# A planner that is told how long DMA transposes take, and loads of a pipeline's start held back and cast on the way in: a two-layer attention and feed-forward kernel

## Chip, cores, metric

One core of one Trainium2 chip. The metric is the device time of one execution in microseconds (us). Each kernel was run several times, and every kernel that is compared ran on the same chip in turns with the kernel before. All runs used here are of the normal ("fast") state. A ratio is the mean time of one kernel's fast runs over the mean of the other's of the same rounds, with a 95% interval, so it is not quite the ratio of the medians quoted beside it. The rounds ran on different chips, so kernels of different rounds are compared by their ratios to before.

## The reference

Two identical layers on x of 1 x 2048 x 576 (bfloat16), cut to what matters:

```
x = x + attention(layernorm(x))     # 32 heads of 18, causal, window of 256 keys
x = x + feed_forward(layernorm(x))  # 576 -> 4608, gelu, 4608 -> 576, biases b1, b2
# and both once more with the same weights
```

## The kernel before

The tokens go through in chunks of 512 (four tiles of 128 rows); two layers of four chunks make eight, k = 0 to 7. For a chunk there are these pieces, and the kernel interleaves the pieces of neighbouring chunks so that TensorE always has something to do:

- `qkv(k)`: projections of the normalised and transposed chunk (`xnTa`), 24 groups of 5 matmuls; results are cast by VectorE (DVE) and transposed by DMA into `qT`, `kT`;
- `E(k)`: attention in eight groups of four heads, in two halves (k,0) and (k,1): scores on TensorE, exp on ScalarE (ACT), causal and window masks on GpSimd (POOL, `affine_select`), values matmul on TensorE, normalisation on DVE into `attq`;
- `tail(k)`: `attq` is transposed by DMA into `attT`, the output projection is added to the residual `x_res`, and the result is normalised and transposed (`xnTm`);
- `G(k,h)` and `mm2(k,h)`, h = 0, 1: the two halves of the feed-forward, first matmul with GELU on ACT, second matmul added to `x_res`.

Almost no engine order is written by hand (only ACT's work, and scores and first feed-forward matmuls among each other, keep the order in which the program states them). Every instruction is a task with a believed duration (`cost`), a believed extra time until its result is there (`lat`) and a priority. A list scheduler in the host program takes, again and again, the task that could start first by these beliefs, and of equals the one with the lower priority number. The order that comes of it is fixed in the program; semaphores keep it correct. So a wrong belief never gives a wrong result: it puts an instruction too early in the queue of its engine, which then stands and waits with work behind it that was ready.

```python
            free[t.eng] = st + t.cost
            t.end = st + t.cost + t.lat
    ...
        # every DMA transpose, in ln_norm_T, qkv and tail:
        add("sp", lambda e: e.dma_start_transpose(...), ..., dma="t", ring=8, cost=1.3, lat=1.4, prio=...)
    ...
    # the start: x, q/k/v weights, x again, wo, all at once
    x_load(0, n0, [], 4.0, -10)               # plain loads into x_in, a view of hT
    for n, w in enumerate("qkv"):
        dma("act", wqkv[...], ..., lat=7.0 + 3 * n, prio=-10, fifo="act")
    for a in range(n0, NT, 4):
        x_load(a, min(4, NT - a), ["wkA"], 4.0 + (a - n0) * 0.75, -10)
    dma("act", wo_sb[...], ..., lat=14.0, ...)
    ...
    for t in range(NT):                       # residual in float32, cast by POOL
        add("pool", lambda e, t=t: e.tensor_copy(x_res[:, t, :], x_in[:, t, :]), ...)
    for i in range(n0):
        qkv(0, i, -5)
    for t in range(n0, NT):                   # statistics of all later tiles
        ln_stats(t, -1, x_in, f"xin{t}")
    ln1(1, -0.9)
    ...
    for _ in range(NB1):                      # feed-forward weights, as soon as q of chunk 0 is there
        w1_load(0, [f"q{n0 - 1}"])
    w2_load(0, 0, [f"q{n0 - 1}"])
    ...
    # in tail(k), after the normalisation of a tile:
            add("pool", lambda e, t=t: e.tensor_tensor(x_res[:, t, :], x_res[:, t, :], b2bc[:, :], ALU.add),
                reads=["b2"], writes=X(t), cost=1.4, prio=prio + 0.9)
```

The softmax here doesn't subtract the row's maximum and nothing guards it: scores larger than these inputs give would overflow.

## Time and profile before

| | before |
|---|---|
| median of 3 runs | 1006.06 us (1005.98 to 1006.28) |
| TensorE busy (profiled run) | 927.4 of 1007.7 us |
| TensorE waits for `attT` | 16.8 us in 9 pieces |
| first matmul | 15.01 us |

How to read it: PE is TensorE's matmuls, PEld its weight loads; a busy share near 1 means that only idle time, and time in which TensorE runs at a lower clock, can be won. The page's first lines, and the row of its 40-slice table that gives the granted clock in tenths (each slice is 25 us):

```profile
span 1007.7 us, 22352 instructions
PE 927.4 (92%) x9312; PEld 584.9 (58%) x9312; DVE 311.9 (31%) x771; ACT 586.2 (58%) x705; POOL 378.4 (38%) x519
...
PE   3596799899999999899998999999999999999998
...
PEclk9786799999999999999998999999999999999999
```

The first five slices belong to the ramp, the start of the run until its stages repeat: PE shows 3, 5, 9, 6 and 7 there, at a lower clock. From the sixth slice on PE shows 8 or 9 in every slice.

The view of waits, for PE alone (what ended each idle piece; us in total, times, longest):

```profile
engine line waited for: us in total, times, longest us
PE ps L519 <- DMA xnTa<-xn: 25.3, 4, 15.0
PE ps L519 <- DMA attT<-attq: 16.8, 9, 3.6
PE ps L589 <- ACT pT L598: 12.2, 22, 1.3
```

L519 is a matmul of `qkv` or of the output projection; the tile name tells which. The 25.3 us for `xnTa` lie in the ramp (15.0 of them before the first matmul); the waits for `attT` are nine pieces in eight chunks, spread over the run after 133 us. The timeline of PE in one of the repeating stages shows what such a wait does (start, length, what, and in brackets the idle time before it):

```profile
773.24 0.29 PE L525 MATMUL ps<-wqkv,xnTa 128*128 128x288 bf16 x1
...
773.85 0.29 PE L525 MATMUL ps<-wqkv,xnTa 128*128 128x288 bf16 x1
776.18 0.67 PE L519 MATMUL ps<-wo_sb,attT 128*128 128x288 bf16 x4 [2.04 <-DMA attT<-attq]
...
777.63 0.45 PE L525 MATMUL ps<-wo_sb,attT 128*128 128x288 bf16 x1
```

TensorE stands for 2.04 us until the first `attT` transpose lands, then runs the first tile. SP's queue in the same trace has the four `attT` transposes issued from 771.64 us. The last matmul of `qkv` ended at 774.14 us (773.85 + 0.29), 2.5 us after the issue; the data came 4.5 us after it. The planner believed 1.3 + 1.4 = 2.7 us (`cost` and `lat`).

### The profile page before, as it was taken

The numbers are of one execution on the slowest core, as the hardware profiler recorded it, in microseconds if no ns is written. First come the engines' busy times: TensorE is split into PE (matmuls) and PEld (weight loads), VectorE is DVE, ScalarE is ACT, GpSimd is POOL, SyncE is SP. The second block draws the span as 40 slices with busy tenths as digits, with TensorE's granted clock in tenths as the row PEclk, the third lists the DMA queues.
The fourth block names the chain that finished last, engine by engine and source line by source line (L and its number), as shares of the span: only waits on it lengthen the run. The fifth ranks groups of instructions, "written<-read, shape, count | busy, mean of one in ns | idle before, by whom it ended". The sixth has DMA issues, their size and how long they took to land.

```text
span 1007.7 us, 22352 instructions
## 1 busy us (share of the span) xinstructions
PE 927.4 (92%) x9312; PEld 584.9 (58%) x9312; DVE 311.9 (31%) x771; ACT 586.2 (58%) x705; POOL 378.4 (38%) x519
## 2 busy tenths in 40 slices
PE   3596799899999999899998999999999999999998
PEld 2363556556565656656575565755566565656556
DVE  4742611342136211534036130361114410132001
ACT  0356568577753777447761687627774377852531
POOL 8445724354333434425153161533333342541000
PEclk9786799999999999999998999999999999999999
DMA  9925220974268251881628633484517725074540
GB/s 252 273 45 89 54 72 25 199 187 131 72 150 164 75 163 39 180 184 41 183 70 170 148 108 94 120 177 103 166 48 170 143 66 183 25 194 122 184 129 25
DMA packets 226757, 126.60 MB, mean 126 GB/s; under 512 B 141792, under 2 KB 226528, under 8 KB 226656
## 3 DMA queue, kind: packets, MB, share of 16 engines
q1 hardware_dynamic: 219456, 122.20, 49.0%
q10 hardware_dynamic: 2432, 2.65, 0.9%
q0 software_dynamic: 4768, 0.31, 0.8%
q8 instruction: 74, 1.21, 0.5%
q14 instruction: 27, 0.22, 0.1%
HBM read 90.10 MB, written 2.36 MB: 92 GB/s over the span
## 4 chain that ended last, share of the span: by engine, by line
PE 68%; DMA 4%; DVE 3%; ACT 3%; issue 1%; POOL 1%; SPq 0%; DVEq 0%
PE ps L737 26%; PE ps L712 24%; PE ps L519 6%; PE ps L636 6%; PE ps L589 4%; DMA attT<-attq 3%; ACT pT L598 2%; PE ps L525 1%; DVE x_res L670 1%; DMA xnTm<-xn 1%; POOL rstd L460 1%; DVE xn L470 1%; ACT hT L716 1%; DVE st_all L447 0%; ACT L753 0%
## 5 line engine op out<-in xcount | busy, mean ns | idle before, releaser
L619 POOL TENSOR_SCALAR_AFFINE_SELECT pT<-pT 128x512 bf16<-128x512 bf16 (+1 forms) x368 | 278.1, 778 | 409.6 <-ACT pT L598 385.3
L598 ACT ACTIVATE pT<-ps 128x1024 bf16<-128x1024 f32 (+2 forms) x384 | 347.2, 971 | 133.6 <-PE ps L589 132.2
L716 ACT ACTIVATE hT<-ps,b1col 128x512 bf16<-128x512 f32 x288 | 196.6, 687 | 262.6 <-PE ps L712 262.4
L737 PE MATMUL ps<-w_sb,hT 128*128 128x288 bf16 x2304 | 314.2, 286 | 6.7 <-DVE x_res L670 5.6
L712 PE MATMUL ps<-xnTm,w_sb 128*128 128x512 bf16 x1440 | 320.1, 379 | 0.1
L737 PEld LDWEIGHTS ps<-w_sb,hT 128*128 128x128 bf16 x2304 | 210.3, 97 | 80.7 <-issue 20.5
L712 PEld LDWEIGHTS ps<-xnTm,w_sb 128*128 128x128 bf16 x1440 | 139.6, 98 | 158.6 <-issue 0.2
L670 DVE TENSOR_TENSOR x_res<-ps,x_res 128x288 f32<-128x288 f32 x160 | 71.0, 450 | 399.9 <-PE ps L737 362.4
L519 PE MATMUL ps<-wqkv,xnTa 128*128 128x288 bf16 x768 | 127.7, 297 | 29.7 <-DMA xnTa<-xn 25.3
L636 PEld LDWEIGHTS ps<-vA,pT 128*128 128x128 bf16 x2880 | 94.4, 96 | 29.1 <-issue 11.2
L519 PEld LDWEIGHTS ps<-wqkv,xnTa 128*128 128x128 bf16 x768 | 73.1, 101 | 58.5 <-issue 18.8
L636 PE MATMUL ps<-vA,pT 128*128 128x20 bf16 x2880 | 100.5, 172 | 5.3 <-POOL pT L619 3.8
L589 PE MATMUL ps<-qT,kT 32*128 32x384 bf16 (+2 forms) x1408 | 76.5, 285 | 18.7 <-ACT pT L598 12.2
L555 DVE CAST qn<-ps 128x288 bf16<-128x288 f32 x128 | 57.0, 452 | 55.2 <-PE ps L525 50.0
L519 PE MATMUL ps<-wo_sb,attT 128*128 128x288 bf16 x256 | 45.9, 313 | 16.8 <-DMA attT<-attq 16.8
L525 PE MATMUL ps<-wqkv,xnTa 128*128 128x288 bf16 x192 | 56.8, 296 | 0.0
L589 PEld LDWEIGHTS ps<-qT,kT 32*128 32x128 bf16 x1408 | 22.6, 93 | 53.9 <-issue 30.0
L694 POOL TENSOR_TENSOR x_res<-x_res,b2bc 128x576 f32<-128x576 f32 x32 | 45.0, 1409 | 15.1 <-DVE xn L470 13.9
L673 DVE TENSOR_TENSOR xn<-ps,x_res 128x288 bf16<-128x288 f32 x32 | 14.6, 457 | 114.7 <-PE ps L737 114.7
L470 DVE TENSOR_SCALAR xn<-x_res,mv_all,rstd 128x576 bf16<-128x576 f32 x60 | 43.1, 723 | 22.1 <-POOL rstd L460 10.4
L458 POOL TENSOR_SCALAR vtmp<-mv_all 128x1 f32<-128x1 f32 (+1 forms) x43 | 8.6, 200 | 103.6 <-DVE mv_all L449 101.2
L519 PEld LDWEIGHTS ps<-wo_sb,attT 128*128 128x128 bf16 x256 | 26.2, 106 | 30.7 <-DMA attT<-attq 20.6
(29 smaller groups left out, 281.5 us busy)
## 6 DMA issues: line engine op xcount, KB each, us to landing
w_sb<-in_B_w_dram SPq DMA_DIRECT2D x144, 288.0 KB, 5.2
w_sb<-in_B_w_dram SPq DMA_DIRECT2D x72, 512.0 KB, 4.2
w_sb<-in_B_w_dram SPq DMA_DIRECT2D x72, 64.0 KB, 3.9
hT<-in_A_x_dram SPq DMA_DIRECT2D x4, 576.0 KB, 6.3
out_dram<-xn SPq DMA_DIRECT2D x16, 144.0 KB, 1.8
wqkv<-in_A_wqkv_dram ACTq DMA_DIRECT2D x3, 576.0 KB, 7.4
wo_sb<-in_A_wo_dram ACTq DMA_DIRECT2D x1, 576.0 KB, 9.6
xnTa<-xn SPq DMA_TRANSPOSE x32, 3.9
```

Source lines behind the costliest of these rows:

```text
L470: add("dve", lambda e: e.tensor_scalar(xn[:, sl, 0:D], s[:, t, :], mv_all[:, t, 0:1], rstd[:, t:t + 1], op0=ALU.subtract, op1=ALU.mult), r ...
L519: ins = e.matmul(bank(bs[o])[:, 0:n], lhs(o, c, full), rhs(o, c, full), start=(c == 0), stop=False)
L525: ins = e.matmul(bank(bs[o])[:, 0:n], lhs(o, 4, full), rhs(o, 4, full), start=False, stop=True)
L555: add("dve", lambda e, o=o, b=bs[o], qv=qv: e.tensor_copy(qv[:, o * 16:(o + 1) * 16, 0:DH], bank(b)[:, 0:HB].rearrange("p (h d) -> p h d", ...
L589: ins = e.matmul(two(bs[j // 2])[:, j % 2, col:col + nq * 128], kT[32 * j:32 * j + 32, g, (T0 + so) % KS, :], qT[32 * j:32 * j + 32, g, qo ...
L598: add("act", lambda e, h2=h2: e.activation(pT[:, sl, 2 * h2:2 * h2 + 2, lo:hi], two(bs[h2])[:, :, lo:hi], ACT.Exp, scale=SCALE), reads=[bs ...
L619: add("pool", lambda e, ap=ap, pat=pat, sgn=sgn, kind=kind: e.affine_select(ap, ap, pattern=pat, compare_op=(ALU.is_ge if kind == "d" else ...
L636: ins = e.matmul(bank(B_O)[:, o:o + VW], pT[:, sl, j, col + qi * 128:col + (qi + 1) * 128], vA[:, (T0 + so) % VS, 4 * g + j, :], start=(fi ...
L670: add("dve", lambda e: e.tensor_tensor(x_res[:, t, sl], bank(b)[:, 0:HB], x_res[:, t, sl], ALU.add), reads=[b], writes=[f"x{t}h{hh}"], cos ...
L712: ins = e.matmul(bank(bk)[:, 0:n], w1_sb[:, sl, col:col + 128], xnTm[:, k % 2, c, 0:n], start=(c == 0), stop=(c == KD - 1))
L716: add("act", lambda e, f=f, fl=fl, bk=bk: e.activation(hT[:, fl, 0:n], bank(bk)[:, 0:n], ACT.Gelu_apprx_tanh, bias=b1col[:, f:f + 1]), rea ...
L737: ins = e.matmul(bank(b)[:, 0:HB], hT[:, fl, i * 128:(i + 1) * 128], w2_sb[:, fl, hh * HB:(hh + 1) * HB], start=(fl == 0), stop=(fl == NFH ...
```

## The change

Its intent: give the planner a truer picture of DMA, and clear the start of the kernel of transfers that nobody needs yet. The core of the diff:

```diff
+            if t.dma is not None:                       # one DMA queue in the plan
+                dma_free = max(dma_free, st + t.cost) + t.move
+                t.lat = max(t.lat, dma_free + 1.3 - st - t.cost)
             t.end = st + t.cost + t.lat
...
     def dma(q, out_, in_, ...):
-        add(q, ..., **kw)                               # latencies given by hand
+        add(q, ..., lat=1.3, move=n / 270e3, **kw)      # n: bytes written
...
-            ... dma="t", ring=8, cost=1.3, lat=1.4, ...             # xn, q, k transposes
+            ... dma="t", ring=8, cost=1.3, lat=2.5, move=0.6, ...
-            reads=rd + ["aqd"], ... lat=1.4, prio=prio - 0.1)       # attT transposes
+            reads=rd + ["aqd"], ... lat=4.0, move=0.6, prio=prio - 0.1)
...
+    def x_load(a, cnt, reads, prio):                    # bf16 -> float32 on the way, issued by POOL
+        dma("pool", x_res[:, a:a + cnt, :], x_dram[...], reads=reads, ..., cls="xr", ...)
-    (x of all chunks, wo, q/k/v weights at once; POOL casts; statistics of all tiles in one block)
+    w_load(0); w_load(1)
+    x_load(chunk 1, [f"xa{n0 - 1}"])   # after chunk 0's last transpose
+    w_load(2, ["xa0"])                 # v weights after its first
+    x_load(chunk 0, [f"k{n0 - 1}"])
+    stats0(1)                          # statistics chunk by chunk
+    # in E(0): wo after group 0, x of chunk 2 after group 1, w1 blocks after groups 3, 5, 7
+    # in G(0,0): w2 pair by pair behind the GELUs, x of chunk 3 after the seventh GELU
-            ... x_res + b2 on POOL: prio=prio + 0.9
+            ... prio=prio + 3
-        memset of qn: all columns
+        memset of qn: only the padding columns
```

More of the change, by code (lines that the diff above doesn't have):

```diff
@@ L158 @@
 class Task:
-    __slots__ = ("idx", "eng", "fn", "reads", "writes", "cost", "lat", "prio", "dma", "ring", "handles", "alloc",
+    __slots__ = ("idx", "eng", "fn", "reads", "writes", "cost", "lat", "prio", "dma", "ring", "handles", "alloc", "move",
                  "npred", "succ", "ready", "end", "plain")
@@ L194, in __init__, with add @@
         self.fifo_last = {}
-    def add(self, eng, fn, reads=(), writes=(), dma=None, ring=4, cost=0.1, lat=0.1, prio=0.0, alloc=(), fifo=None, plain=False, after=()):
+    def add(self, eng, fn, reads=(), writes=(), dma=None, ring=4, cost=0.1, lat=0.1, prio=0.0, alloc=(), fifo=None, plain=False, after=(), move=0.0):
         t = Task(idx=len(self.tasks), eng=eng, fn=fn, reads=tuple(reads), writes=tuple(writes), cost=cost, lat=lat, prio=prio,
                  dma=dma, ring=ring, alloc=tuple(alloc), handles=tuple({r for r in tuple(reads) + tuple(writes) if isinstance(r, Bank)}),
-                 plain=plain)
+                 plain=plain, move=move)
         pred = set()
@@ L260, in schedule @@
         order = []
+        dma_free = 0.0
         n = len(self.tasks)
@@ L398, in dma @@
     def dma(q, out_, in_, reads=(), writes=(), cls="w", ring=8, **kw):
-        add(q, lambda e: e.dma_start(out_, in_), reads=reads, writes=writes, dma=cls, ring=ring, **kw)
-    def x_load(a, n, reads, lat, prio):
-        dma("sp", x_in[:, a:a + n, :], x_dram[a * P:(a + n) * P, :].rearrange("(t p) d -> p t d", p=P), reads=reads,
-            writes=[f"xin{t}" for t in range(a, a + n)], cls="x", ring=4, cost=0.6, lat=lat, prio=prio)
+        n = 2 if cls != "xr" else 4
+        for s in out_.shape:
+            n *= s
@@ L405, in build_kernel @@
+        add(q, lambda e: e.dma_start(out_, in_), reads=reads, writes=writes, dma=cls, ring=ring, lat=1.3, move=n / 270e3, **kw)
     n0 = CH[0][2]
-    x_load(0, n0, [], 4.0, -10)
-    for n, w in enumerate("qkv"):
-        dma("act", wqkv[:, 0:4, n * D:(n + 1) * D], A_wqkv[0:512, n * D:(n + 1) * D].rearrange("(c p) d -> p c d", p=P),
-            writes=[f"w{w}A"], lat=7.0 + 3 * n, prio=-10, fifo="act")
-        dma("act", wqkv[0:64, 4, n * D:(n + 1) * D], A_wqkv[512:576, n * D:(n + 1) * D], writes=[f"w{w}B"], lat=7.0 + 3 * n, prio=-10,
-            fifo="act")
-        if PAIR:
-            dma("act", wqkv[64:128, 4, n * D:(n + 1) * D], A_wqkv[512:576, n * D:(n + 1) * D], writes=[f"w{w}C"], lat=7.0 + 3 * n,
-                prio=-10, fifo="act")
@@ L415, in build_kernel @@
-    for a in range(n0, NT, 4):
-        x_load(a, min(4, NT - a), ["wkA"], 4.0 + (a - n0) * 0.75, -10)
-    dma("act", wo_sb[:, 0:4, :], A_wo[0:512, :].rearrange("(c p) d -> p c d", p=P), writes=["woA"], lat=14.0, prio=-10, fifo="act")
-    dma("act", wo_sb[0:64, 4, :], A_wo[512:576, :], writes=["woB"], lat=14.0, prio=-10, fifo="act")
-    if PAIR:
-        dma("act", wo_sb[64:128, 4, :], A_wo[512:576, :], writes=["woC"], lat=14.0, prio=-10, fifo="act")
+    dma("sp", x_in[:, 0:n0, :], x_dram[0:n0 * P, :].rearrange("(t p) d -> p t d", p=P), writes=[f"xin{t}" for t in range(n0)], cls="x",
+        ring=4, cost=0.6, prio=-10)
@@ new lines, in w_load @@
+    def w_load(n, reads=()):
+        w = "qkv"[n]
+        dma("act", wqkv[:, 0:4, n * D:(n + 1) * D], A_wqkv[0:512, n * D:(n + 1) * D].rearrange("(c p) d -> p c d", p=P), reads=reads,
+            writes=[f"w{w}A"], cost=0.6, prio=-10, fifo="act")
+        dma("act", wqkv[0:64, 4, n * D:(n + 1) * D], A_wqkv[512:576, n * D:(n + 1) * D], reads=reads, writes=[f"w{w}B"], cost=0.6, prio=-10,
+            fifo="act")
+    def x_load(a, cnt, reads, prio):
+        dma("pool", x_res[:, a:a + cnt, :], x_dram[a * P:(a + cnt) * P, :].rearrange("(t p) d -> p t d", p=P), reads=reads,
+            writes=[r for t in range(a, a + cnt) for r in X(t)], cls="xr", ring=8, cost=1.2, prio=prio)
@@ L422, in build_kernel @@
+    w_load(0)
+    w_load(1)
     add("pool", lambda e: e.memset(nhalf[:, :], -0.5), writes=["nhalf"], cost=0.1, prio=-10)
@@ L426, in build_kernel @@
     for i in range(NQN):
-        add("pool", lambda e, i=i: e.memset(qn[:, i, :], 0.0), writes=[f"qn{i}h{h}" for h in range(2)], cost=1.0, prio=-9)
+        add("pool", lambda e, i=i: e.memset(qn[:, i, :].rearrange("p (h e) -> p h e", e=32)[:, :, DH:32], 0.0),
+            writes=[f"qn{i}h{h}" for h in range(2)], cost=0.5, prio=-9)
     if not PAIR:
@@ L433, in build_kernel @@
     dma("pool", b2bc[:, :], bass.AP(tensor=B_b2.tensor, offset=B_b2.offset, ap=[[0, P], [1, D]]), writes=["b2"], cls="b", ring=2,
-        cost=1.0, lat=4.0, prio=-7)
+        cost=1.0, prio=-7)
     def load_b1(e):
@@ L479, in ln_norm_T @@
         add("sp", lambda e: e.dma_start_transpose(dst[:, :, i * 128:(i + 1) * 128], xn[:, sl, :]),
-            reads=rd, writes=[f"{dname}{i}"], dma="t", ring=8, cost=1.3, lat=1.4, prio=prio)
+            reads=rd, writes=[f"{dname}{i}"], dma="t", ring=8, cost=1.3, lat=2.5, move=0.6, prio=prio)
     w1n = [0]
@@ L493, in w1_load @@
         dma("sp", w1_sb[:, sl, 0:2048].rearrange("p (c f) -> p c f", c=4), B_w1[0:512, cols].rearrange("(c p) f -> p c f", p=P),
-            reads=reads, writes=[f"w1a{sl}"], cls="w1", cost=0.5, lat=4.0, prio=prio)
+            reads=reads, writes=[f"w1a{sl}"], cls="w1", cost=0.5, prio=prio)
         if PAIR:
@@ L498, in w1_load, with w2_load @@
                 dma("sp", w1_sb[64 * b:64 * b + 64, sl, 2048:2304].rearrange("p (a f) -> p a f", a=2), src[:, b],
-                    writes=[f"w1b{sl}_{b}"], cls="w1", cost=0.5, lat=4.0, prio=prio)
+                    writes=[f"w1b{sl}_{b}"], cls="w1", cost=0.5, prio=prio)
         else:
-            dma("sp", w1_sb[0:64, sl, 2048:2560], B_w1[512:576, cols], reads=["w1Z"], writes=[f"w1b{sl}_0"], cls="w1", cost=0.5, lat=4.0,
+            dma("sp", w1_sb[0:64, sl, 2048:2560], B_w1[512:576, cols], reads=["w1Z"], writes=[f"w1b{sl}_0"], cls="w1", cost=0.5,
                 prio=prio)
-    def w2_load(hf, prio, reads=()):
+    def w2_load(hf, prio, gate=False):
         for pr in range(NFH // 2):
@@ L507, in w2_load @@
             dma("sp", w2_sb[:, 2 * pr:2 * pr + 2, :], B_w2[f0 * P:(f0 + 2) * P, :].rearrange("(w p) d -> p w d", p=P),
-                reads=reads, writes=[f"w2s{pr}"], cls="w2", ring=9, cost=0.6, lat=4.0, prio=prio)
+                reads=[f"h{2 * pr}"] if gate else [], writes=[f"w2s{pr}"], cls="w2", ring=9, cost=0.6, prio=prio)
     def two_out(lhs, rhs, n, reads, prio, after=()):
@@ L562, in qkv @@
                 add("sp", lambda e, dst=dst, sl=sl: e.dma_start_transpose(dst, qn[:, sl, :]),
-                    reads=[f"qn{sl}h0", f"qn{sl}h1"], writes=[dn], dma="t", ring=8, cost=1.3, lat=1.4, prio=prio)
+                    reads=[f"qn{sl}h0", f"qn{sl}h1"], writes=[dn], dma="t", ring=8, cost=1.3, lat=2.5, move=0.6, prio=prio)
     def units_of(k):
@@ L683, in tail @@
             add("sp", lambda e, i=i: e.dma_start_transpose(attT[:, :, i * 128:(i + 1) * 128], attq[:, i, :]),
-                reads=rd + ["aqd"], writes=[f"aT{i}"], dma="t", ring=8, cost=1.3, lat=1.4, prio=prio - 0.1)
+                reads=rd + ["aqd"], writes=[f"aT{i}"], dma="t", ring=8, cost=1.3, lat=4.0, move=0.6, prio=prio - 0.1)
         for i in range(nt):
@@ L694, in tail @@
             add("pool", lambda e, t=t: e.tensor_tensor(x_res[:, t, :], x_res[:, t, :], b2bc[:, :], ALU.add),
-                reads=["b2"], writes=X(t), cost=1.4, prio=prio + 0.9)
+                reads=["b2"], writes=X(t), cost=1.4, prio=prio + 3)
     def G_part(k, hf, prio):
@@ L743, in mm2 @@
             if fin:
-                dma("sp", out_dram[t * P:(t + 1) * P, :], xn[:, osl, 0:D], reads=[f"xn{osl}", f"xd{osl}"], cls="o", ring=4, cost=0.5, lat=2.0,
+                dma("sp", out_dram[t * P:(t + 1) * P, :], xn[:, osl, 0:D], reads=[f"xn{osl}", f"xd{osl}"], cls="o", ring=4, cost=0.5,
                     prio=prio)
@@ L769, in build_kernel, with stats0, wo_load @@
         ln_norm_T(i, i, xnTa, "xa", -6, x_in, f"xin{i}")
-    for t in range(NT):
-        add("pool", lambda e, t=t: e.tensor_copy(x_res[:, t, :], x_in[:, t, :]), reads=[f"xin{t}"], writes=X(t), cost=0.7,
-            prio=-2 if t >= n0 else -4)
+    x_load(CH[1][1], CH[1][2], [f"xa{n0 - 1}"], -6)
+    w_load(2, ["xa0"])
     for i in range(n0):
         qkv(0, i, -5)
-    for t in range(n0, NT):
-        ln_stats(t, -1, x_in, f"xin{t}")
+    x_load(0, n0, [f"k{n0 - 1}"], -4)
+    def stats0(k):
+        l, t0, nt = CH[k]
+        for t in range(t0, t0 + nt):
+            ln_stats(t, 4 * k - 5)
+    stats0(1)
     ln1(1, -0.9)
-    add("pool", lambda e: e.memset(fence[:, :], 0.0), reads=[f"xin{t}" for t in range(NT)], writes=[f"h{f}" for f in range(NFH)],
+    add("pool", lambda e: e.memset(fence[:, :], 0.0), reads=[f"xin{t}" for t in range(n0)], writes=[f"h{f}" for f in range(NFH)],
         cost=0.1, prio=-4)
-    for _ in range(NB1):
-        w1_load(0, [f"q{n0 - 1}"])
-    w2_load(0, 0, [f"q{n0 - 1}"])
+    def wo_load():
+        dma("act", wo_sb[:, 0:4, :], A_wo[0:512, :].rearrange("(c p) d -> p c d", p=P), reads=["aq0"], writes=["woA"], cost=0.6, fifo="act")
+        dma("act", wo_sb[0:64, 4, :], A_wo[512:576, :], reads=["aq0"], writes=["woB"], cost=0.6, fifo="act")
+    later = [k for k in range(2, NK) if CH[k][0] == 0]
     for k in range(NK + 1):
@@ L790, in build_kernel @@
             E(k, range(0, 4), b - 0.5)
+            if k == 0:
+                wo_load()
+                kk = later[0]
+                x_load(CH[kk][1], CH[kk][2], ["aq1"], 0)
+                stats0(kk)
+                w1_load(-1, ["aq3"])
         if k >= 2:
@@ L795, in build_kernel @@
             G_part(k - 1, 0, b + 1)
+        if k == 1:
+            w2_load(0, 1, True)
+            for n, kk in enumerate(later[1:]):
+                x_load(CH[kk][1], CH[kk][2], [f"h{6 + 6 * n}"], b + 2)
+                stats0(kk)
         if not last:
             E(k, range(4, 8), b + 1.5)
+            if k == 0:
+                w1_load(-1, ["aq5"])
+                w1_load(-1, ["aq7"])
         if k >= 1:
@@ L805, in build_kernel @@
             tail(k, b + 1.9)
+            if k == 0:
+                w1_load(-1, ["xm0_0"])
         if k >= 1:
```

## The prediction

> **What bounds it now.** TensorE: the page has PE busy 927 of 1007.7 us. A new order can win only the 80 us of idle and the time at a low clock. Idle by stretches (busy time per window): first matmul at 15.0 us; 1.9 to 34.0; 13.4 to 53.8 at clock 0.56; 9.4 to 94.2 at 0.80; 6.7 to 133.4 (the first feed-forward matmul) at 0.78; 34 after. The ramp thus holds 46 us of idle and some 15 us (estimate from busy time and clock) lost to slow matmuls (0.44 us against 0.29 for a 128x288). The Trainium skill ("TensorE: Matmul & The Clock Gate", Part 1) says the clock halves after an idle window of about 3.4 us; the trace agrees: 0.50 after the 7.8 us wait at 44 us.
>
> **Where the ramp loses.** (a) The first matmul waits for a transpose issued at 9.6 us, with v weights, wo and more x tiles in flight; PE waits again (1.8 us) at 22. (b) VectorE does all 12 later tiles' statistics in one block (30 to 41 us), so chunk 1's transposes are issued at 44.6, behind thirteen w1/w2 loads (35.5 to 44.5 us, 350 to 390 GB/s): the 7.8 us wait. "DMA: Bandwidth & Descriptors" (Queues, rings and completion order) says each SDMA engine consumes an issuer's ring in order; the late transposes agree. (c) E(0), chunk 0's attention, has 35.8 us of exp on ScalarE but takes 60. (d) From 103 to 116 us four x_res+b2 adds (1.4 us each) on POOL stand between the mask selects.
>
> **What the change does.** v weights wait for the first transpose, wo for the first attention group; w1 goes block by block during E(0), w2 pair by pair during the first feed-forward. Later x chunks come by casting DMAs on POOL's queue: 16 casts of 0.62 us go (10 us, off the path), about 1 us of descriptor work per load (estimate from b2's 0.8 us) comes, written bytes double. Statistics go chunk by chunk; b2 adds move behind the masks. The planner believes longer transposes (2.5, 4.0 us; trace: 2.6 to 3.9) and a DMA queue, so it should fill the wait before the output projection.
>
> **Sum (estimates).** First matmul at 11.5, no second wait: -4. The 7.8 us wait and its cold matmuls: -9. Tighter E(0), warmer clock, freer masks: -9. First feed-forward matmul at 111 instead of 133. Afterwards the waits for attT (16.8 us in nine pieces) and their neighbours halve: -7. Against it: nine w2 loads (2.6 MB), four w1 blocks (2.4 MB) and an x chunk in the first feed-forward's 18 us, near 390 GB/s: +3; planner accidents +2. Total -24.
>
> **Prediction: 982 us, 8 in 10 between 964 and 998.** Faster by over 2% (under 985.9): 0.60; within 2%: 0.37; slower: 0.03.
>
> **What would show it.** The 15.0 and 7.8 us waits for xnTa become about 11 and under 2; idle before the first feed-forward matmul falls from 46 to about 28 us, and the clock of slices 2 to 5 rises. Waits for attT after the ramp fall below 9 us. PE busy falls to about 915. POOL's cast group disappears. DMA share nears 1 in the first feed-forward.
>
> **What would make it wrong.** SP issues in order: a held-back load released later than planned blocks transposes behind it. Slow casting DMAs (before has none) would delay chunk 1. Exp (36+23 us for E(0) and half of E(1)) may bound the ramp and keep the clock low. Work moved out of the ramp may only return later. If the steady order does not improve: about 990.

## The result

| | before | after |
|---|---|---|
| median | 1006.02 us (4 runs) | 990.62 us (989.61 to 993.21, 4 runs) |
| ratio | | 0.9855 (0.9832 to 0.9879) |
| TensorE busy | 927.4 us | 919.6 us |
| first matmul | 15.01 us | 14.47 us |
| TensorE waits for `attT` | 16.8 us | 4.3 us |

The changed kernel ran once more in a later round: 990.75 us, ratio 0.984 (0.9817 to 0.9863). It is 15.4 us faster by the first medians, inside the predicted range. It is not faster by over 2%, to which the prediction had given 0.60; "within 2%" had 0.37.

The profile after, the same lines (the line numbers have moved: L523 was L519, L593 was L589):

```profile
span 991.5 us, 22315 instructions
PE 919.6 (93%) x9263; PEld 583.4 (59%) x9312; DVE 317.2 (32%) x771; ACT 585.8 (59%) x705; POOL 369.4 (37%) x507
...
PE   4676699999999999999999999999999999999998
...
PEclk9795799999999999999999999999999999999999
```

The view of waits of after, PE alone (columns as before):

```profile
PE ps L593 <- ACT pT L602: 18.3, 28, 1.4
PE ps L523 <- DMA xnTa<-xn: 14.7, 2, 14.5
PE ps L640 <- POOL pT L623: 7.6, 6, 3.0
PE ps L640 <- DVE attq L655: 4.5, 1, 4.5
PE ps L523 <- DMA attT<-attq: 4.3, 4, 1.7
```

The waits for `attT` are nearly gone. In the ramp only the wait before the first matmul is left of those for `xnTa`, but waits for exp, masks and `attq` have come in their place, and the clock digits of the first slices are no better. In the stage shown above the projection now comes later in TensorE's order, behind more `qkv` groups, and nothing waits:

```profile
764.90 0.29 PE L529 MATMUL ps<-wqkv,xnTa 128*128 128x288 bf16 x1
765.26 0.66 PE L523 MATMUL ps<-wo_sb,attT 128*128 128x288 bf16 x4
765.76 0.29 PE L529 MATMUL ps<-wo_sb,attT 128*128 128x288 bf16 x1
```

SP issued the first of these transposes at 760.87 us in this trace, 4.4 us ahead of the projection's first matmul.

**Where the 16 us came from.** Two traces can only be compared between points at which the same work has been done. The obvious mark, the start of the first feed-forward (133.36 us before, 124.93 after), is not such a point: before, 100 of chunk 2's 120 `qkv` matmuls had been done by the first GELU, after, only 50; at 0.12 us each (0.65 us for four and 0.29 for the fifth, which overlap to 0.61 a group) the missing 50 are 6 us of work. At the first matmul of `mm2(0,1)` the counts of matmuls of all kinds agree again, in these two traces and in those of all experiments (but for the matmuls that e10 adds). The ramp is counted up to this mark from here on. It started at 213.18 us before and at 209.45 after. So the ramp gave 3.7 us, and the repeating stages the other 12.5 of the 16.2 us between these two profiled runs. The windows between such marks, before and after (length, busy time with counts for PE, PEld, DVE, ACT, POOL, then clock, DMA share, GB/s):

```profile
core 0: us, PE busy (x) PEld busy (x) DVE busy (x) ACT busy (x) POOL busy (x), PEclk, DMA share, GB/s
15.01:34.39 19.38, 17.48 (x124) 12.54 (x124) 13.45 (x36) 0.00 (x0) 9.21 (x17) 1.00 1.47 206
34.39:94.83 60.44, 37.61 (x540) 23.73 (x540) 25.24 (x70) 35.82 (x48) 32.17 (x46) 0.71 0.56 132
94.83:153.61 58.78, 52.11 (x519) 30.79 (x519) 23.93 (x56) 36.07 (x43) 27.91 (x36) 0.86 0.30 70
153.61:213.18 59.57, 55.00 (x590) 34.34 (x583) 19.57 (x47) 37.92 (x45) 27.16 (x36) 1.00 0.66 146
213.18:1007.70 794.52, 765.16 (x7555) 483.43 (x7548) 222.40 (x545) 475.12 (x570) 268.98 (x360) 0.99 0.48 123
```

The same windows of after:

```profile
14.47:32.07 17.60, 17.55 (x124) 12.75 (x124) 10.61 (x25) 0.00 (x0) 0.82 (x1) 1.00 1.11 204
32.07:88.26 56.19, 37.94 (x540) 24.19 (x540) 25.83 (x69) 35.61 (x49) 32.75 (x46) 0.72 0.62 132
88.26:145.36 57.10, 45.66 (x465) 25.51 (x468) 25.24 (x58) 35.91 (x43) 28.83 (x37) 0.80 0.59 142
145.36:209.45 64.09, 60.60 (x639) 39.58 (x633) 24.95 (x59) 37.85 (x45) 28.53 (x38) 1.00 0.67 145
209.45:991.50 782.05, 757.86 (x7511) 481.31 (x7548) 223.44 (x544) 475.13 (x570) 269.02 (x360) 1.00 0.50 126
```

The marks are: first matmul; first exp; first exp of chunk 1; first `mm2(0,0)` matmul; first `mm2(0,1)` matmul; end. The third window is 1.7 us shorter with 50 fewer `qkv` matmuls in it (the table shows 54 fewer records, as some are missing), and its idle time went up from 6.7 to 11.4 us; the fourth is 4.5 us longer because the 50 matmuls came back there. The last window is 12.5 us shorter. (49 of the 9,312 matmul records are missing from this trace of after, so its split into busy and idle is not exact; the lengths are. The second trace of the same kernel, after_again, is complete and shows 11.2 us of idle time in the third window.)

How far can one profile be trusted? The profiled run of after was the slowest of its four, that of after_again the fastest of its four. They differ by 0.8 us at `mm2(0,1)` and by 2.7 us from there to the end, and the waits for `attT` are 4.3 us in one and 0.6 in the other. Differences of that size between single profiles show nothing.

### The profile page after: what moved, and what is told of

It reads as the page before. It is cut to its first block, busy times and chain, and to the rows that moved or that the text cites. A ratio compares the mean times of both kernels' runs of the same rounds, so it can differ in the third digit from the quotient of the medians.

```text
span 991.5 us, 22315 instructions
## 1 busy us (share of the span) xinstructions
PE 919.6 (93%) x9263; PEld 583.4 (59%) x9312; DVE 317.2 (32%) x771; ACT 585.8 (59%) x705; POOL 369.4 (37%) x507
## 4 chain that ended last, share of the span: by engine, by line
PE 80%; DMA 5%; DVE 4%; ACT 4%; issue 3%; POOL 3%; SPq 1%; DVEq 0%; POOLq 0%
PE ps L741 28%; PE ps L716 27%; PE ps L523 10%; PE ps L640 7%; PE ps L593 6%; ACT pT L602 3%; DMA attT<-attq 2%; PE ps L529 2%; DVE x_res L674 1%; DVE st_all L451 1%; POOL rstd L464 1%; POOL pT L623 1%; DMA xnTa<-xn 1%; DMA x_res<-in_A_x_dram 1%; ACT hT L720 1%
## 5 line engine op out<-in xcount | busy, mean ns | idle before, releaser
L716 PE MATMUL ps<-xnTm,w_sb 128*128 128x512 bf16 x1391 | 312.6, 379 | 3.2 <-ACT pT L602 0.6
L523 PE MATMUL ps<-wqkv,xnTa 128*128 128x288 bf16 x768 | 127.1, 296 | 18.7 <-DMA xnTa<-xn 14.7
L640 PEld LDWEIGHTS ps<-vA,pT 128*128 128x128 bf16 x2880 | 94.6, 97 | 38.1 <-issue 15.5
L523 PEld LDWEIGHTS ps<-wqkv,xnTa 128*128 128x128 bf16 x768 | 73.7, 101 | 44.8 <-issue 15.0
L593 PE MATMUL ps<-qT,kT 32*128 32x384 bf16 (+2 forms) x1408 | 77.6, 289 | 23.6 <-ACT pT L602 18.3
L593 PEld LDWEIGHTS ps<-qT,kT 32*128 32x128 bf16 x1408 | 22.7, 93 | 60.5 <-issue 28.8
L474 DVE TENSOR_SCALAR xn<-x_res,mv_all,rstd 128x576 bf16<-128x576 f32 x60 | 46.8, 796 | 26.2 <-POOL rstd L464 13.8
L451 DVE BATCH_NORM_STATS2 st_all<-x_res 128x6 f32<-128x288 f32 x120 | 50.7, 445 | 13.7 <-DMA x_res<-in_A_x_dram 12.4
L698 POOL TENSOR_TENSOR x_res<-x_res,b2bc 128x576 f32<-128x576 f32 x32 | 45.3, 1416 | 13.9 <-DVE xn L474 12.5
L650 DVE RECIPROCAL rinv<-ps 128x16 f32<-128x16 f32 x64 | 16.4, 257 | 95.6 <-PE ps L640 95.5
```

Source lines behind the costliest of these rows:

```text
L451: add("dve", lambda e, i=i, s=s: e.bn_stats(st_all[:, t, i, :], s[:, t, i * HB:(i + 1) * HB]), reads=res, writes=[f"st{t}_{i}"], cost=0.43 ...
L523: ins = e.matmul(bank(bs[o])[:, 0:n], lhs(o, c, full), rhs(o, c, full), start=(c == 0), stop=False)
L593: ins = e.matmul(two(bs[j // 2])[:, j % 2, col:col + nq * 128], kT[32 * j:32 * j + 32, g, (T0 + so) % KS, :], qT[32 * j:32 * j + 32, g, qo ...
L640: ins = e.matmul(bank(B_O)[:, o:o + VW], pT[:, sl, j, col + qi * 128:col + (qi + 1) * 128], vA[:, (T0 + so) % VS, 4 * g + j, :], start=(fi ...
L716: ins = e.matmul(bank(bk)[:, 0:n], w1_sb[:, sl, col:col + 128], xnTm[:, k % 2, c, 0:n], start=(c == 0), stop=(c == KD - 1))
```

## The experiments

Three questions were left: which part of the change gave the gain of the repeating stages; why the ramp, of which 22 us were expected (at the first feed-forward matmul), gave 3.7; and whether the parts that did not pay can be made to. The marks of all kernels (us in the profiled run; start of the first matmul, of the first exp, of chunk 1's first exp, and of `mm2(0,1)`, and the time from there to the end):

| kernel | first matmul | first exp | E(1) starts | mm2(0,1) | rest | `attT` waits | ratio to before |
|---|---|---|---|---|---|---|---|
| before | 15.0 | 34.4 | 94.8 | 213.2 | 794.5 | 16.8 | 1 |
| after | 14.5 | 32.1 | 88.3 | 209.4 | 782.0 | 4.3 | 0.9855 |
| after again | 14.4 | 32.3 | 87.6 | 208.6 | 779.3 | 0.6 | 0.984 |
| e1 planner alone | 21.5 | 38.1 | 89.2 | 207.2 | 780.3 | 3.0 | 0.9817 |
| e2 loads alone | 14.4 | 37.7 | 90.5 | 212.5 | 796.9 | 17.0 | 1.001 |
| e3 three latencies alone | 15.2 | 36.1 | 92.4 | 211.4 | 779.1 | 1.1 | 0.9843 |
| e5 `attT` latency alone | 14.8 | 34.1 | 95.4 | 213.3 | 780.5 | 1.9 | 0.9881 |
| e6 the two others alone | 15.0 | 34.2 | 93.0 | 211.3 | 791.0 | 16.0 | 0.9986 |
| e4 after, chunk 1 free | 14.4 | 32.8 | 83.3 | 204.6 | 780.2 | 1.9 | 0.9806 |
| e7 e4, b2 adds late | 14.5 | 32.6 | 83.9 | 207.1 | 775.5 | 2.2 | 0.9766 |
| e8 e7, b1 load late | 16.8 | 33.7 | 83.6 | 206.0 | 774.9 | 2.2 | 0.9745 |
| e9 e1, b2 adds late | 21.8 | 38.9 | 89.9 | 210.6 | 775.0 | 3.4 | 0.9787 |

All ran in five rounds, and all but one gave the correct result (the one is said).

### e1_planner: the planner's part on the old loads

```diff
 (kernel before)
+            if t.dma is not None:
+                dma_free = max(dma_free, st + t.cost) + t.move
+                t.lat = max(t.lat, dma_free + 1.3 - st - t.cost)
+        kw["lat"] = 1.3            # in dma(), with move = bytes / 270e3
-  lat=1.4                          # the transposes
+  lat=2.5, move=0.6  (attT: lat=4.0, move=0.6)
```

> The kernel before with the planner's part alone: the DMA queue in the plan, bytes as time, transposes believed to take 2.5, 2.5 and 4.0 us; loads, casts and gates as before. Theory P (the change gains in the repeating stages, because matmuls are put before the output projection): 12 us of the 15.5 come from the planner, so about 994 us, and the waits for attT after the ramp fall from 16.8 us to under 6; the start of chunk 1's second feed-forward half (mm2 (0,1), 213.2 us in before) moves by under 4 us. Rival L (the gain comes from the staged loads of the ramp): under 4 us faster, 1002 us or more.

Measured: 989.59 us against 1007.56, ratio 0.9817 (0.9792 to 0.9842), waits for `attT` 3.0 us. The planner's part alone gives the whole gain; its interval overlaps that of the full change. Theory L falls. Theory P holds for the repeating stages (780.3 us against 794.5), but its bound on the ramp does not: the planner alone moved `mm2(0,1)` by 6.0 us, not under 4. It did so although its first matmul came at 21.5 us, 6.5 us later than before. So a later first matmul need not make the kernel later, although an earlier one was one of the terms of the prediction. (The order differs from before in other places too, so this does not show what the start alone is worth.)

### e2_loads: the gates, stages and casting DMAs with the old beliefs

```diff
 (kernel after)
-                dma_free = ...; t.lat = max(...)
-  lat=2.5, move=0.6  (attT: lat=4.0, move=0.6)
+  lat=1.4
-  lat=1.3, move=n / 270e3
+  fixed latencies of 2 to 7 us by kind of load (before: 2 to 14)
```

> The changed kernel with the planner's beliefs of before (transposes 1.4 us, fixed load latencies, no DMA queue); gates, staging and casting DMAs stay. Theory P: only the ramp's part is left, about 4 us, so about 1002 us, and attT waits of about 15 us after the ramp come back. Rival L: 12 us or more faster than before, 994 or less. If both e1 and e2 gain little, the two parts need each other.

Measured: 1009.01 us against 1007.56, ratio 1.001 (0.9986 to 1.0034). Even the 4 us left to them by theory P are not there: `mm2(0,1)` starts 0.7 us earlier, and the rest takes 2.4 us longer, both within what two profiles of one kernel differ by. The waits for `attT` are back:

```profile
PE ps L522 <- DMA attT<-attq: 17.0, 9, 4.0
```

### e3_lat: three numbers

```diff
 (kernel before)
-  lat=1.4   # xn, q, k transposes
+  lat=2.5
-  lat=1.4   # attT transposes
+  lat=4.0
```

> The kernel before with nothing but the three numbers for the transposes' latency (1.4 to 2.5, 2.5, 4.0). Theory P1 (the believed latency is what moves the output projection back): nearly all of e1's gain, within 3 us of it. Theory P2 (the queue model, by which a transpose planned behind a burst of loads is late, is needed): less than half of e1's gain.

Measured: 992.35 us against 1007.56, ratio 0.9843 (0.9816 to 0.987); e1 had 0.9817 in the same rounds, 2.8 us lower by the medians. Theory P1 holds: the believed latency does it. Whether the queue model adds anything is not shown in the total, as the intervals overlap; in the profiled runs `mm2(0,1)` comes at 211.4 us against 207.2, and from there on the two take the same time within the difference of two profiles (779.1 and 780.3).

### e5_att4 and e6_rest25: the numbers apart

```diff
 e5 (kernel before)
-  lat=1.4   # attT transposes
+  lat=4.0
 e6 (kernel before)
-  lat=1.4   # xn, q, k transposes
+  lat=2.5
```

> The kernel before with one number changed: the believed latency of the attT transposes, 1.4 to 4.0. Theory A (only the wait before the output projection cost time): most of the 15 us that the three numbers gave, so 995 us or less, and attT waits near 1 us. Theory B (the other transposes' belief does as much, by moving q/k/v work): 4 to 8 us faster only.

> The kernel before with the other two numbers alone: the transposes of normalised x, q and k believed to take 2.5 instead of 1.4, attT still 1.4. Theory A: under 4 us faster, and attT waits stay near 16 us. Theory B: 7 us or more faster.

Measured: e5 994.87 us, ratio 0.9881 (0.9854 to 0.9908), waits for `attT` 1.9 us; e6 1004.86 us, ratio 0.9986 (0.996 to 1.0013), waits 16.0 us. Theory A holds in both: one number gives 12 us, where the whole change gave 15.4 in its own rounds. The line of the wait in e5:

```profile
PE ps L519 <- DMA attT<-attq: 1.9, 3, 0.9
```

The ramp of e5 is that of before to within 0.2 us at `mm2(0,1)`. From there on the waits for `attT` fell from 13.1 to 1.9 us, and this part of the run from 794.5 to 780.5: TensorE's idle time by 9.2 us (other waits grew a little) and its busy time, for the same matmuls, by 4.8. The busy time went because before has two stretches at half clock in this part, 6.8 us from 534.6 and 3.4 us from 776.9, each beginning during or just after a wait for `attT` (of 3.6 us until 535.5 and of 2.04 us until 776.2); e5 has none before the end. What the number 4.0 stands for was not tested further: with `cost` the planner now believes 5.3 us, more than the 4.5 seen above, so its worth may lie in being long enough and not in being exact.

### e4_x1_free: chunk 1 no longer held back

```diff
 (kernel after)
-    x_load(CH[1][1], CH[1][2], [f"xa{n0 - 1}"], -6)
+    x_load(CH[1][1], CH[1][2], [], -6)
```

Why: in the trace of after, POOL issued chunk 1's load only when chunk 0's last transpose had landed, and from 31.7 us to chunk 1's first `qkv` matmul TensorE had nothing but `E(0)` (the timeline of POOL in after):

```profile
20.64 0.82 POOL L406 DMA_DIRECT2D x_res<-in_A_x_dram  x1 [7.87 <-DMA xnTa<-xn]
...
35.52 0.19 POOL L462 TENSOR_SCALAR vtmp<-mv_all 128x4 f32<-128x4 f32 x1 [0.63 <-DVE mv_all L453]
36.52 0.81 POOL L406 DMA_DIRECT2D x_res<-in_A_x_dram  x1 [0.81 <-DMA kT<-qn]
37.36 1.05 POOL L464 TENSOR_TENSOR rstd<-vtmp,nhalf 128x4 f32<-128x4 f32 x1
```

The load was issued at 20.64 us; its statistics could begin at 28.5. Then the variance was there at 35.5, but POOL's next instruction was another casting load that waited for chunk 0's last `kT`, and the rstd behind it came at 37.4. Chunk 1's first `qkv` matmul came at 44.29 us (51.57 before).

> The changed kernel with chunk 1's casting load no longer held back until the last transpose of chunk 0 has landed (it was issued at 20.6 us); the planner puts it two instructions earlier on POOL, about 11 us. Theory A (the ramp gained little because chunk 1 arrives late: its first matmul came at 44.3 us after 12.6 us with little for TensorE): chunk 1's first matmul at about 37 us and 3 to 6 us faster in all. Theory B (exp on ScalarE and the cold clock bound the ramp): chunk 1's first matmul earlier, but the whole within 1.5 us. Theory C (the load collides with the transposes of chunk 0): the first score matmul (31.7 us) later by 2 us or more.

Measured: 988.95 us against 1007.56, ratio 0.9806 (0.978 to 0.9832). Chunk 1's first matmul came at 35.2 us, 9.1 us earlier (37 was expected), and `mm2(0,1)` at 204.6, 4.8 us earlier than in after. (After has 0.9855 and 0.984 in rounds of its own; the intervals just overlap, so the total alone would not prove it.) Theory A holds in its size; the first score matmul moved by 0.7 us only, so C does not show here. But 9.1 us of earlier data gave 4.8: of chunk 1's 120 `qkv` matmuls, which fill TensorE's time between the pieces of `E(0)`, 110 now run in its first half (92 in after) and only 10 are left for the second.

### e7_b2late: the b2 adds out of the way

The prediction had read the change of priority as moving the four adds behind the masks. The trace of after shows that it did not (first POOL; each line has the start, the length, engine, line and operation):

```profile
104.83 0.63 POOL L623 TENSOR_SCALAR_AFFINE_SELECT pT<-pT 128x512 bf16<-128x512 bf16 x1
105.44 0.55 POOL L464 TENSOR_TENSOR rstd<-vtmp,nhalf 128x1 f32<-128x1 f32 x1
105.94 1.41 POOL L698 TENSOR_TENSOR x_res<-x_res,b2bc 128x576 f32<-128x576 f32 x1
107.44 0.28 POOL L462 TENSOR_SCALAR vtmp<-mv_all 128x1 f32<-128x1 f32 x1
107.79 0.64 POOL L623 TENSOR_SCALAR_AFFINE_SELECT pT<-pT 128x512 bf16<-128x512 bf16 x1
```

DVE in the same stretch:

```profile
105.36 0.23 DVE L650 RECIPROCAL rinv<-ps 128x16 f32<-128x16 f32 x1
...
106.02 1.65 DVE L474 TENSOR_SCALAR xn<-x_res,mv_all,rstd 128x576 bf16<-128x576 f32 x1 [0.34 <-POOL rstd L464]
107.59 0.45 DVE L655 TENSOR_TENSOR attq<-ps,rinv 128x288 bf16<-128x288 f32 x1
```

A priority decides only between tasks that could start at the same believed time, so the planner believed that nothing else on POOL could start earlier than this add. While POOL does its 1.41 us add, DVE's normalisation of a tile takes 1.65 us instead of the usual 0.58 (median of 60), and the multiplication that gives `attq`, behind it in DVE's queue, starts at 107.59. TensorE waits 4.50 us for it. The Trainium skill ("SBUF — State Buffer", SBUF: two separate sides) says that DVE in some modes and GpSimd share one port pair, an exclusive lock held for the whole instruction; these lines agree: the normalisation ended 0.3 us after the add did (107.67 and 107.35).

```diff
 (e4)
-  in tail(k): x_res + b2, reads=["b2"], prio=prio + 3
+  after G_part(k - 1, 0, b + 1), for the tiles of chunk k - 1: x_res + b2, reads=["b2", "h6"], prio=b + 1
```

> The run with chunk 1's load free, and the x_res+b2 adds on POOL made to wait for the seventh GELU of the chunk's own feed-forward. The intended priority change had left them among the mask selects (101 to 113 us). If they are what makes VectorE and so TensorE wait (the 4.5 us wait for attq at 104 us), that wait goes under 1.5 us, and the start of chunk 0's second feed-forward half comes 3 to 6 us earlier than the 204.6 us of that run; the whole about 985. If exp and the cold clock bound this stretch, under 1 us.

Measured: 984.31 us against 1006.97, ratio 0.9766 (0.9736 to 0.9796). The size was as expected and the place was not: TensorE still waits 3.6 us for `attq` in the ramp, `mm2(0,1)` comes 2.4 us later than in e4, and the gain is in the repeating stages, 775.5 us against 780.2. e9 below shows the same 5 us there. (The intervals of e4 and e7 overlap, so the total alone would not show a gain.)

The traces say what the 5 us are. The same collision stands in repeating stages of after (lines of POOL, DVE and PE together, `qn` being the cast of a `qkv` result):

```profile
308.45 1.40 POOL L698 TENSOR_TENSOR x_res<-x_res,b2bc 128x576 f32<-128x576 f32 x1
308.58 1.59 DVE L474 TENSOR_SCALAR xn<-x_res,mv_all,rstd 128x576 bf16<-128x576 f32 x1 [0.50 <-POOL rstd L464]
310.09 1.17 DVE L559 CAST qn<-ps 128x288 bf16<-128x288 f32 x3
310.59 0.67 PE L523 MATMUL ps<-wqkv,xnTa 128*128 128x288 bf16 x4 [0.98 <-DVE qn L559]
```

The normalisation again ends 0.3 us after the add, the cast behind it in DVE's queue is late, and TensorE waits 0.98 us for it. After `mm2(0,1)` such waits for `qn` add up to 4.9 us in e4 and 4.2 in e1; in e7, e8 and e9 none is listed. The 2.4 us by which `mm2(0,1)` came later than in e4 are nearly all one stretch at half clock, from 144.9 to 151.8 us, which e4 does not have; TensorE's waits for exp between `mm2(0,0)` and this mark are 2.9 us in both. Why the clock fell in one and not in the other was not found.

### e8_b1late: the start of POOL's queue

In after the first rstd waits behind the descriptor work of the b1 load (4,608 single elements, written as float32):

```profile
7.37 0.19 POOL L462 TENSOR_SCALAR vtmp<-mv_all 128x1 f32<-128x1 f32 x1 [2.24 <-DVE mv_all L453]
7.62 1.90 POOL L443 DMA_DIRECT2D b1col<-in_B_b_dram  x1
9.56 0.59 POOL L464 TENSOR_TENSOR rstd<-vtmp,nhalf 128x1 f32<-128x1 f32 x1
```

So the first transpose was issued at 10.63 us, 1.0 us later than before, although POOL had less to clear at the start.

```diff
 (e7)
-  load_b1 first on POOL, no reads
+  load_b1 after the set-up of chunk 0, reads=["rstd3"]
-  x_load(chunk 1, [])
+  x_load(chunk 1, ["rstd1"])
```

> The run before this one, with the b1 load (1.9 us of descriptor work on POOL, standing between the first variance and its rstd) put behind chunk 0's last rstd, and chunk 1's load behind the second variance. First transpose about 9.3 us instead of 10.6, first matmul 13.0 to 13.5 instead of 14.4. If the start is on the path, 1 us faster in all; a run with the first matmul at 21.5 us was no slower than others, which speaks for less than 1 us.

Measured: 980.75 us against 1006.97, ratio 0.9745 (0.9716 to 0.9773); e7's interval overlaps it. The first transpose was issued at 9.58 us, as meant, but landed at 16.7: the casting load of chunk 1 went out at 9.66 and b1 at 12.30, and the first transpose, in flight beside them, took 7.1 us instead of 3.6 (e7). So the first matmul came at 16.8 us, not at the 13.0 to 13.5 expected and 2.3 us later than in e7, and the kernel was not slower for it. This is the fastest correct kernel, 26 us under the kernel before in the same rounds.

### e9_planner_b2late: does staging help at all?

```diff
 (e1, on the loads of before)
+  the same move of the b2 adds as in e7
```

> The changed kernel itself, unedited, to stand beside the next two on one chip: ratio 0.985 to 0.987, as first measured. If it comes out at 0.982 or less, the earlier 0.9855 and the planner's 0.9817 do not differ and the staged loads are simply neutral on top of the planner; if it stays at 0.985 or more, they cost some 4 us on top of it.

> The planner's part alone on the loads of before (no gates, no casting DMAs; ratio 0.9817 when measured), with the b2 adds held until the seventh GELU. Theory N (staging and casting add nothing once the planner knows the latencies): the adds give the same 4 us here, ratio 0.977 to 0.979. Theory S (staging is needed for the rest): ratio 0.980 or more.

Measured: after again 990.75 us, ratio 0.984 (0.9817 to 0.9863), between the two cases named, so whether the staged loads cost anything on top of the planner stays open. e9: 985.56 us, ratio 0.9787 (0.976 to 0.9814). Between N and S the number falls to N, though its interval reaches into S. With the b2 adds late, the plain loads of before reach 0.9787, and the staged, cast, freed loads 0.9766 (e7) and 0.9745 (e8). The intervals overlap, so a gain of the staging is not shown in the total; in the profiled runs `mm2(0,1)` starts 3.5 us (e7) and 4.6 us (e8) before that of e9.

### e10_warm and e11_halfexp: what bounds the second half of E(0)?

With all but 10 of chunk 1's `qkv` matmuls done, this piece lasts 24.4 us in e8 with TensorE busy 14.2 at a clock of 0.54, ACT 17.7 and POOL 16.4. e10 repeats every score matmul of this piece three times into the same place, for a warm clock; e11 leaves out half of its exp, with a wrong result.

```diff
 e10 (e8)
-            for (so, qo, nq, col) in parts:
+            for (so, qo, nq, col) in parts * (3 if k == 0 and g >= 4 else 1):
 e11 (e8)
-            activation(pT[:, sl, 2 * h2:2 * h2 + 2, lo:hi], two(bs[h2])[:, :, lo:hi], Exp)
+            activation(pT[:, sl, 2 * h2:2 * h2 + nj, lo:hi], two(bs[h2])[:, 0:nj, lo:hi], Exp)   # nj = 1 here
```

> The run with b1 late and chunk 1 free (980.75 us), with every score matmul of chunk 0's groups 4 to 7 done three times into the same place, same result: useless work that keeps TensorE busy from 59 to 84 us, where its clock was 0.54, it worked 14.4 of 24.6 us, and exp 17.6. If the low clock is what stretches this exp-bound piece, the clock goes over 0.8, the piece shrinks by 2 to 4 us, the whole to about 978. If the piece is bound by the chain scores, exp, mask, values whatever the clock, no change within 1 us; if the added matmuls stay cold, they bound it and it is 3 us or more slower.

> The run with b1 late and chunk 1 free, with a wrong result on purpose: in chunk 0's groups 4 to 7 exp is done for two of the four heads of a group only, which takes some 8.5 us off ScalarE's 17.8 us of work between 59.2 and 83.6 us; the order of all engines is the same. If exp bounds this piece of the ramp, it shrinks by 5 us or more, and chunk 1's first exp (83.6 us) comes at 79 or earlier. If the chain from scores over exp and POOL's masks to the values matmuls or POOL itself (16.7 us busy) bounds it, it shrinks by under 3 us.

The windows from the first exp of the piece to chunk 1's first exp (columns as in the windows above); first e8:

```profile
59.23:83.62 24.39, 14.24 (x246) 8.38 (x246) 6.08 (x19) 17.71 (x24) 16.43 (x25) 0.54 0.59 125
```

e10:

```profile
61.18:88.97 27.79, 21.16 (x366) 11.59 (x366) 5.71 (x17) 18.14 (x24) 15.87 (x24) 0.54 0.50 107
```

e11:

```profile
59.03:81.81 22.78, 14.41 (x246) 8.41 (x246) 6.15 (x19) 10.46 (x24) 16.28 (x25) 0.50 0.61 134
```

e10 (986.72 us, ratio 0.98 (0.9775 to 0.9824)) had TensorE busy for 21.2 of 27.8 us and the clock stayed at 0.54: the added matmuls ran cold and the piece grew by 3.4 us. So it did not answer what a warm clock would be worth. e11 (981.0 us, ratio 0.9752 (0.973 to 0.9774), relative error 0.28) took 7.2 us off ACT and the piece shrank by 1.6 us. Exp is not what bounds most of it. A lack of filler does not seem to either: the piece lasts 24.4 us with 10 `qkv` matmuls in it (e8), 25.7 with 28 (after) and 26.2 with 50 (before). What is left is either POOL's masks (16.3 of 22.8 us in e11) or the chain from scores over exp and masks to values and on to chunk 1's `qT`; the two were not told apart.

## Why the prediction was right or wrong

The time, 990.6 us, lies in the range (964 to 998), and the direction was right, but the gain was 15.4 us and not 24, and the range holds by errors that partly cancel: the ramp was put 18 us too high, the repeating stages 5.5 too low, and the 5 us set against the gain did not show as costs of their own. It is luck, too, that the prediction names about 990 for the case that the steady order does not improve: 990.6 came out, with the steady order improved and the ramp not.

- **The repeating stages: mis-sized, too small.** "Afterwards the waits for attT (16.8 us in nine pieces) and their neighbours halve: -7." They fell from 16.8 to 4.3 us, and this part of the run became 12.5 us shorter. The mechanism was right, and e5 shows it alone: one believed latency, 12 us. The waits also cost more than themselves in this part of the run (in e5 11.2 us of waits and 14.0 us of time), because matmuls after two of them ran at half clock, 0.45 us instead of 0.29.
- **The ramp: mis-sized, far too large; this is the step that failed.** "First feed-forward matmul at 111 instead of 133" was worth 22 us in the sum. It came at 124.9, and with 50 matmuls put off; at equal work the ramp gave 3.7 us. Its three terms:
  - "First matmul at 11.5, no second wait: -4." It came at 14.47, since b1's descriptor work stood in POOL's queue before the first rstd. The second wait is gone and the first exp came 2.3 us earlier. But a start at 21.5 us in e1 and at 16.8 in e8 did not show in the total.
  - "The 7.8 us wait and its cold matmuls: -9." The wait is gone and chunk 1's first matmul came 7.3 us earlier, but the hold-back itself now delayed it; freeing it gave 4.8 us more (e4). And the cold matmuls were not this wait's doing: in before the granted clock was halved from 36.2 us on, 7.6 us before the wait began and after 3.4 us in which TensorE was 43% busy; in after, without the wait, it was halved from 36.3 us on. So no idle window came before it. From 20 us on half clock took 51.2 us of the ramp before and 54.7 after, with waits for exp and masks in the place of the one that went.
  - "Tighter E(0), warmer clock, freer masks: -9." The adds stayed among the masks, and the idle time between chunk 1's first exp and `mm2(0,0)` rose by 4.8 us (6.7 to 11.4).
- **The burst in the first feed-forward: +3.** DMA did reach a share of 1.04 from 130 to 150 us (the view's share can exceed 1), but no wait for weights shows there, and from the first feed-forward matmul to the first of `mm2(0,0)` it took 20.3 us before and 20.4 after.
- **"Work moved out of the ramp may only return later"** stood among the risks, and it did.
- **"PE busy falls to about 915"**: 919.6. "... idle before the first feed-forward matmul falls from 46 to about 28 us": to 44.
- "Slow casting DMAs (before has none)": before has two small ones, since the b1 and b2 loads turn bfloat16 into float32 as well. Of the large ones the gate of the first cost 4.8 us (e4); what the slowness of the cast itself cost was not tested.
- What the prediction did not ask is whether the two halves of the change are both needed. They are not: the loads alone give nothing (e2), the planner alone gives it all (e1).

## What to carry to other kernels

In a kernel whose order comes from a list scheduler, look first for the producer whose believed latency is furthest below the one in the trace, and for the engine that waits for it in every stage: here one number, 1.4 to 4.0, was worth 12 us. When one wait is gone, look for the next one in the same stage: here an add on POOL whose DVE neighbour made TensorE wait for a cast, 5 us. Hold back a load only as long as its consumer is really late in the queue, and check afterwards whether the gate has become the wait. Compare two schedules at points where the same instructions have been executed; an earlier start of a stage can be work put off.

## What the Trainium skill lacked or had wrong

- "DMA: Bandwidth & Descriptors" states bandwidth for DMA transposes but no time from issue to landing for small ones within SBUF: medians here were 2.6 to 3.9 us per 128-row tile before and 3.3 to 3.5 after, 4.5 us for the first `attT` of the row of four shown above, and 7.1 us for a first `xnTa` with loads in flight (e8). The planner's belief about this latency, not the bandwidth, was worth 12 us.
- The same page says that casting DMAs go through GpSimd but gives no time for them. Its fit for the GpSimd path would give 4.7 us (an estimate, from bytes written); the four of 1,152 KB written in after took 5.7 to 7.9 us from issue to landing, beside other traffic, and 0.8 us of POOL to issue.
- "TensorE: Matmul & The Clock Gate" describes the clock as following how busy TensorE has been. Here a stretch with score matmuls of 32 rows (e10) had TensorE 76% busy (21.2 of 27.8 us) and was granted 0.54, while `qkv` matmuls of 128 rows went from 0.44 to 0.29 us each within 5 us of their start (14.5 to 19.2 us in after). Apart from transposes on TensorE, the page does not say which matmuls count as busy.
